# Attention and two expert layers on one core: magnitude from the ratio, range checks moved to the experts, a planner that knows a shared port, three sets of tiles, and a state product in strips

## The chip, the cores and the metric

The kernel runs on one core of a Trainium2 chip. The metric is the device time of one execution in microseconds (us), the median of several runs. A core has a matrix engine (TensorE, PE in the rows), VectorE (DVE), ScalarE (ACT), GpSimd (POOL), and SyncE (SP), which here issues most of the DMAs. Each engine works through its own queue in order, and engines wait for one another by semaphores.

## The reference

Three layers follow one another: an attention with complex decays over 4 batches, 8 heads, 768 steps and 48 columns a head; an expert layer with one dense block; and eight experts of which each token takes two.

```python
mag = np.sqrt(a_re * a_re + a_im * a_im)
scale = np.minimum(mag, 0.999) / (mag + 1e-06)
a_re_n, a_im_n = (a_re * scale, a_im * scale)
for t in range(S):
    new_re = ar * S_re - ai * S_im
    new_im = ar * S_im + ai * S_re
    kv = np.einsum('bhd,bhe->bhde', k[:, :, t], v[:, :, t])
    S_re, S_im = (new_re + kv, new_im)
    y[:, :, t] = np.einsum('bhd,bhde->bhe', q[:, :, t], S_re)
# y as x (3072 x 384): h = x @ w_in; solu = h * softmax(h); layer norm; @ w_out
# then 8 experts, two for each token:
    h = np.maximum(x[mask] @ w1[e], 0.0)
    out[mask] += top2_w[mask, k, None] * (h @ w2[e])
```

## The kernel before

The kernel works in four stages: attention, the dense block (MoE1), the routing, and the experts.

**Attention.** The 768 steps of a batch are cut into chunks of 128, 24 chunks in all. Chunks are handled in groups, 13 of them: two of one chunk at the start and eleven of two (`GROUPS0`, `NG`). `Attention.group` writes the steps of a group. Elementwise work on the decays comes first, on tiles of 128 x 384 for each chunk, so 128 x 768 for most groups: `re` clips the real part and keeps its minimum (L387), `imx` takes the largest imaginary part (L389), `im2` and `re2` square both on ScalarE (L392, L393), `sum` adds the squares on GpSimd (L398), `lnm`, `exm` and `l2c` make the logarithm of the clipped magnitude (L399, L400, L402); beside them `lnre` and `exre` make 1/re, `r` the ratio im/re on GpSimd (L397), and `atan` the angle (L405). Per chunk a triangular matrix product sums the angles over time (`sums`, L414, and `next`, L427) and another the logarithms (`decay`, L440). `f` and `fi` are the decay and its inverse (L443, L445), `qf` and `kf` scale q and k by them on GpSimd (L448, L450), `qp` (GpSimd) and `kp` (VectorE) turn them by cosine and sine into 128 x 768 tiles (L481). Then, per chunk, transposes (`tr`, L494) with copies out of PSUM (`hc`, L499 on ScalarE and L501 on VectorE), the scores `pA` (L506), their mask `aT` (L508), the update of the state `pu` (L515, 20 of the 24 chunks) with `add` and `st` (L521 to L526), and the output `py` (L535), copied by `yc` (L542). py is already written in strips of 32 or 16 rows (`Y_PARTS`).

What checks that the numbers are in range runs along with this: `re`, `imx`, a sum kept by `re2`, and a minimum over the high words of the weights (`wmin`, L310). They are put together in `in_range` at expert 1.

Between the steps of attention stand the conversions of MoE1's weights from pairs of 32-bit words (`plan_convert`, 6 pieces of `w_in` and 8 of `w_out`): L291, L303, L296, L305, L306 on VectorE, and for `w_in` also L308 on GpSimd and L309 on VectorE.

**What sets the order.** Each step is an entry of `Plan` with its engine, a cost from `cost()`, what it reads and writes, a due time, and for loads the time on the wire. `Plan.order` is a list scheduler: it takes the engine that could start first, and of its ready entries the one with the least sum of due time, an offset by name (`OFF`, empty before), `WAIT` times the wait, and `PEN` for a switch of ScalarE's table. The order so found is the order of each engine's queue. `PAIR` says which engine does which step. Tiles of `l2`, `m2` and `an` exist in `EWB` sets.

**MoE1, routing and experts.** TensorE's and ScalarE's order is the order of the code. An expert's work is an up product in 16 steps (`bank`, L1165; `hh` on ScalarE, L1167; `hl` on VectorE, L1168) and a down product over seven tiles (L1179). The weights arrive through SP into tiles r (two buffers `r2` for w2) and are split into a high and a low part (`w2_split`, w2l L1141). Rows of x are gathered and results scattered by GpSimd's DMAs.

Of the kernel before, what the change touches and what calls it, by code (L numbers as in the profile page):

```python
# [21 lines left out]
P = 128  # L22
# [4 lines left out]
VW = HD + D  # L27
# [23 lines left out]
ADVJ = {20: [0, 1, 1, 1]}  # L51
ADV2 = [2, 2, 0, 0, 1, 2, 0, 0]
# [12 lines left out]
EWB = 2  # L65
# [4 lines left out]
NW = D2  # L70
# [3 lines left out]
RE_MIN, IM_MAX, RE2_MAX = 0.55, 0.8, 1e12  # L74
# [6 lines left out]
YM = 0.07  # L81
# [12 lines left out]
def convert(tc, cv, raw_src, n, dst, wmin=None):  # L94

# [33 lines left out]
def moe1_f32(tc, wf, cv, w_in, w_out, g_ln, w_gate, w_noise, wmin=None, plan=None, parts=None):  # L129
# [8 lines left out]
    wm = lambda i: None if wmin is None else wmin[:, i:i + 1]  # L138
# [18 lines left out]
    steps = [small]
    for i in range(NWI):
        d, n = divmod(i * CW, FF)
        steps.append(lambda d=d, n=n, i=i: convert(tc, cv, wi32[d, :, n:n + CW], CW, wi[:, d, n:n + CW], wm(i)))  # L160
# [8 lines left out]
def cost(kind, n):  # L169

    fixed, rate = {"V": (0.15, 960), "VV": (0.15, 530), "VC": (0.18, 750), "V2": (0.2, 720), "G": (0.2, 400), "G1": (0.16, 1200), "A": (0.2, 1200), "AP": (0.17, 1200)}[kind]
    return fixed + n / rate


class Plan:
# [6 lines left out]
    def add(self, fn, engine, us, r=(), w=(), new=(), table=None, due=1e9, wire=0.0, after=(), name="", release=0.0):  # L182
# [24 lines left out]
        self.ops.append((fn, engine, us, deps - {k}, order - {k}, table, due, wire, name, release))  # L207
# [7 lines left out]
    def order(self, trace=None):  # L215
# [21 lines left out]
        table, left, done, wire = None, n, [], 0.0  # L237
        while left:
            e = min((x for x in engines if ready[x]), key=lambda x: max(free[x], min(at[k] for k in ready[x])))
            t = max(free[e], min(at[k] for k in ready[e]))  # L240
            best = None
            for k in ready[e]:
                s = max(t, at[k])
# [32 lines left out]
def plan_convert(plan, tc, cv, raw_src, n, dst, wmin, k, due, release, parts=None):  # L276
# [22 lines left out]
    v = v2 = cost("VC", n)  # L299
    add = lambda fn, us, r, w, new=(), e="V": plan.add(fn, e, us, r=r, w=w, new=new, due=due, release=release, name=f"conv{k}.")  # L300
# [9 lines left out]
    add(lambda: V.tensor_reduce(wmin, hi().bitcast(F32), axis=AX.X, op=ALU.min, apply_absolute_value=True), v, (("raw", k),), ())  # L310


class Attention:


    def __init__(self, tc, x5, y, ident, mask, trt, trc, hpi, le6, magic, remin, immax, resum):
        self.tc, self.x5, self.y, self.ident, self.mask, self.trt, self.trc = tc, x5, y, ident, mask, trt, trc
        self.hpi, self.le6, self.magic = hpi, le6, magic
        self.remin, self.immax, self.resum = remin, immax, resum
        self.t, self.pools = {}, {}  # L320

    def open(self, stack):
# [4 lines left out]
        for x in self.vt:  # L327
            G.memset(x[:, :, HD:], 0.0)
        self.sb = [self.sp.tile([D2, VW], F32, name=f"sb{i}") for i in range(2)]
        for x in self.sb:  # L330
            G.memset(x[:, HD:], 0.0)
# [23 lines left out]
    def group(self, plan, g, b, c0, n, sb, psum, load):  # L355
# [22 lines left out]
        def l_v():  # L378
# [8 lines left out]
        ew(lambda: V.tensor_scalar(re(), re(), RE_MIN, None, op0=ALU.max, op1=ALU.min, accum_out=self.remin[:, g:g + 1]),  # L387
           "V", w=(("ri", g),), name="re")
        ew(lambda: V.tensor_reduce(self.immax[:, g:g + 1], im(), axis=AX.XY, op=ALU.max, apply_absolute_value=True),  # L389
           "V", r=(("im", g), ("ld", g)), name="imx", due=due + 8)  # L390
        m2, l2, an = (lambda: x("m2")), (lambda: x("l2")), (lambda: x("an"))
        ew(lambda: A.activation(sb("l2", g, full, EWB)[:, :n], im(), AF.Square), "A", r=(("im", g), ("ld", g)), new=(("l2", g, EWB),), name="im2")  # L392
        ew(lambda: A.activation(sb("m2", g, full, EWB)[:, :n], re(), AF.Square, accum_out=self.resum[:, g:g + 1]),  # L393
           "A", r=(("ri", g), ("ld", g)), new=(("m2", g, EWB),), extra=.09, name="re2")
        ew(lambda: A.activation(re(), re(), AF.Ln), "A", w=(("ri", g),), table=LNEXP, name="lnre")
        ew(lambda: A.activation(re(), re(), AF.Exp, scale=-1.0), "A", w=(("ri", g),), table=LNEXP, name="exre")
        ew(lambda: eng[E("r")].tensor_mul(sb("an", g, full, EWB)[:, :n], im(), re()), E("r"), r=(("ri", g), ("im", g), ("ld", g)), new=(("an", g, EWB),), name="r")  # L397
        ew(lambda: eng[E("sum")].tensor_add(m2(), m2(), l2()), E("sum"), r=(("l2", g),), w=(("m2", g),), name="sum")  # L398
        ew(lambda: A.activation(l2(), m2(), AF.Ln), "A", r=(("m2", g),), w=(("l2", g),), table=LNEXP, name="lnm")  # L399
# [3 lines left out]
           r=(("m2", g),), w=(("l2", g),), name="l2c")  # L403
# [6 lines left out]
        for i in range(n):  # L410
# [24 lines left out]
            ew(abs_, E("ad", i), r=(("d", g, i), ("d", g), ("an", g)), w=(("ad", g, i),), kind=kinds[E("ad", i)], name=f"ad.{i}.", **one)  # L435
# [8 lines left out]
            def fi_(i=i, pcn=pcn):  # L444
# [904 lines left out]
```

## Time and profile before

| | |
|---|---|
| median of 3 runs | 1017.37 us (1014.77 to 1017.72) |
| profiled execution | 1018.7 us, span 1016.9 us, mean granted clock 0.975 |
| attention | 0 to 278 us |
| MoE1 | 278 to 513 us |
| routing, first gathers | 513 to 569 us |
| experts | 569 to 1016.9 us |

The span is what the trace covers, 1.8 us less than the execution's time. Stages overlap a little at their borders; each border above is the time at which TensorE goes over to the next stage's work.

### The profile page before, as it was taken

The page shows a single profiled execution, that of the slowest core. Times are in us where ns is not written, and L with a number is a line of the kernel's source. Part 1 is how long each engine was busy: PE and PEld are TensorE (multiplying, and loading weights), DVE is VectorE, ACT ScalarE, POOL GpSimd, SP SyncE. Part 2 cuts the span into 40 slices and gives each one's busy share as a digit, 9 for nine tenths or more (in the row PEclk, how much of TensorE's full clock was granted, in tenths as well). Part 3 has the DMA queues.
Part 4 walks back from the last instruction along what each step waited for, and adds up shares of the span by engine and source line. Part 5 has one row for each costly group of instructions (what it writes and reads, how often), then busy time and mean ns, then how long its engine had stood idle before and what let it go on. Part 6 is the DMA issues. An engine that isn't in the chain of part 4 may idle for free.

```text
span 1016.9 us, 17137 instructions
## 1 busy us (share of the span) xinstructions
PE 950.5 (93%) x6599; PEld 847.0 (83%) x6599; DVE 613.6 (60%) x1334; ACT 479.5 (47%) x853; POOL 404.8 (40%) x389
## 2 busy tenths in 40 slices
PE   2887999989899999999969999999999999999995
PEld 1665887767789999899867989999898999989895
DVE  5899998997466778778746355343443534344330
ACT  7787888887445455555423243141322314142220
POOL 4476765765320033033225452343625334362411
PEclk9998999999999999999979999999999999999998
DMA  8444633421000000120023334243432424242300
GB/s 260 154 137 142 205 126 115 136 65 47 10 35 24 16 25 25 39 65 26 17 78 78 105 109 142 60 125 105 118 111 77 143 63 149 90 141 68 94 17 33
DMA packets 65545, 90.89 MB, mean 89 GB/s; under 512 B 24299, under 2 KB 54697, under 8 KB 65456
## 3 DMA queue, kind: packets, MB, share of 16 engines
q1 hardware_dynamic: 53984, 65.02, 21.1%
q0 software_dynamic: 11472, 24.70, 7.8%
q8 instruction: 54, 0.88, 0.4%
q14 instruction: 35, 0.29, 0.1%
HBM read 74.82 MB, written 20.16 MB: 93 GB/s over the span
## 4 chain that ended last, share of the span: by engine, by line
PE 80%; DVE 10%; ACT 4%; DMA 2%; POOL 2%; issue 1%; SPq 1%; POOLq 0%; DVEq 0%; ACTq 0%
PE bank L1179 23%; PE bank L1165 21%; PE px L671 10%; PE ph L622 9%; PE tr L494 4%; PE pA L506 3%; PE py L535 3%; PE pu L515 2%; PE pl L659 2%; PE bank L1023 1%; DVE kp L481 1%; POOL qp L481 1%; PE pth L414 1%; ACT L212 1%; DVE aT L508 1%
## 5 line engine op out<-in xcount | busy, mean ns | idle before, releaser
L1179 PE MATMUL bank<-w2h,hh 128*128 128x384 f32 (+1 forms) x448 | 153.6, 343 | 0.0
L1179 PE MATMUL bank<-w2l,hh 128*128 128x384 f32 (+1 forms) x448 | 150.3, 336 | 0.2 <-DVE w2l L1141 0.2
L1179 PE MATMUL bank<-w2h,hl 128*128 128x384 f32 (+1 forms) x448 | 150.4, 336 | 0.0
L1187 POOL DMA_INDIRECT out_dram<-o,slt x56 | 54.9, 980 | 234.5 <-DVE o L1184 211.4
L1168 DVE SCALAR_TENSOR_TENSOR hl<-bank,hh 128x336 fp32r<-128x336 f32 (+1 forms) x128 | 78.2, 611 | 106.2 <-ACT hh L1167 106.2
L1165 PE MATMUL bank<-xh,w1h 128*128 128x512 f32 (+1 forms) x384 | 136.9, 357 | 0.0
L1165 PE MATMUL bank<-xl,w1h 128*128 128x512 f32 (+1 forms) x384 | 136.1, 354 | 0.2 <-DVE xl L1025 0.2
L1165 PE MATMUL bank<-xh,w1l 128*128 128x512 f32 (+1 forms) x384 | 136.1, 354 | 0.0
L1167 ACT ACTIVATE hh<-bank 128x336 fp32r<-128x336 f32 (+1 forms) x128 | 67.2, 525 | 138.0 <-PE bank L1165 137.1
L961 POOL DMA_INDIRECT sld<-rows,sl x48 | 50.3, 1047 | 186.5 <-DVE sl L958 174.0
L1184 DVE SCALAR_TENSOR_TENSOR o<-bank,slt,gp 128x384 f32<-128x384 f32 (+1 forms) x49 | 30.3, 617 | 126.3 <-PE bank L1179 126.3
L1024 ACT ACTIVATE xh<-bank 128x384 fp32r<-128x384 f32 (+1 forms) x52 | 24.0, 474 | 171.8 <-PE bank L1023 171.8
L1179 PEld LDWEIGHTS bank<-w2l,hh 128*128 128x128 f32 (+1 forms) x448 | 81.7, 182 | 2.1 <-DVE w2l L1141 0.5
L1179 PEld LDWEIGHTS bank<-w2h,hh 128*128 128x128 f32 (+1 forms) x448 | 81.6, 182 | 1.5
L1179 PEld LDWEIGHTS bank<-w2h,hl 128*128 128x128 f32 (+1 forms) x448 | 81.5, 182 | 1.6
L1165 PEld LDWEIGHTS bank<-xl,w1h 128*128 128x128 f32 x384 | 72.5, 189 | 8.0 <-DVE xl L1025 0.5
L1165 PEld LDWEIGHTS bank<-xh,w1l 128*128 128x128 f32 x384 | 72.6, 189 | 7.6
L1165 PEld LDWEIGHTS bank<-xh,w1h 128*128 128x128 f32 x384 | 72.3, 188 | 7.8
L671 PE MATMUL px<-woh,ll 128*128 128x400 f32 x192 | 67.0, 349 | 1.1 <-DVE ll L661 1.0
L671 PE MATMUL px<-woh,lh 128*128 128x400 f32 x192 | 66.8, 348 | 0.7 <-ACT lh L660 0.7
L671 PE MATMUL px<-wol,lh 128*128 128x400 f32 x192 | 66.8, 348 | 0.0
L1003 POOL DMA_INDIRECT x<-x2d,slt x56 | 53.5, 955 | 26.6 <-issue 18.9
(254 smaller groups left out, 2207.1 us busy)
## 6 DMA issues: line engine op xcount, KB each, us to landing
r<-in_moe_w_dram SPq DMA_DIRECT2D x24, 512.0 KB, 3.5
r<-in_moe_w_dram SPq DMA_DIRECT2D x32, 384.0 KB, 3.3
ri<-in_x_dram SPq DMA_DIRECT2D x22, 384.0 KB, 3.8
qk<-in_x_dram SPq DMA_DIRECT2D x22, 384.0 KB, 3.7
out_dram<-zero SPq DMA_DIRECT2D x24, 192.0 KB, 5.7
x2d<-xo SPq DMA_DIRECT2D x24, 192.0 KB, 1.8
vt<-in_x_dram SPq DMA_DIRECT2D x11, 384.0 KB, 3.3
raw<-in_moe_w_out_dram SPq DMA_DIRECT2D x8, 384.0 KB
```

The costliest lines, as they stand in the source:

```text
L494: T.transpose(p[:, h, :], t[dst, g][:, i, 4 * hg + h].rearrange("p a d -> p (a d)"), self.ident)
L506: T.matmul(pA[:, h, :], t["kT", 2 * j + hg][:, h, :], t["qT", 2 * j + hg][:, h, :], start=True, stop=True)
L535: T.matmul(t["py", j][32 * k:32 * k + n1 - n0, d], x[:, h * D + n0:h * D + n1], t[a, 2 * j + h // 4][:, h % 4, :], start=a == "aT", stop=T ...
L622: self.tc.nc.tensor.matmul(ph[:, n:n + 512], l[:, d, :], w[:, d, n:n + 512], start=k == 0, stop=k == 3 * ND - 1)
L671: nc.tensor.matmul(px, a[:, f, :], w[:, f, :], start=k == 0, stop=k == 3 * NF - 1)
L961: ins = G.indirect_dma_start(out=sld, out_offset=bass.IndirectOffsetOnAxis(ap=sl[:, i, kk:kk + 1], axis=0), in_=rows[:, j0 + i, kk, :], in ...
L1003: G.indirect_dma_start(out=x[:m_], out_offset=None, in_=x2d[:rows_known], in_offset=bass.IndirectOffsetOnAxis(ap=o.sl[:m_, i, 0:1], axis=0))
L1165: T.matmul(p[:, :n], wt[:, fs], xx[:, d, :], start=kc == 0, stop=kc == 3 * ND - 1)
L1167: A.activation(o.hh[s][:, f, :], p[:, :n], AF.Relu)
L1168: V.scalar_tensor_tensor(o.hl[s][:, f, :], p[:, :n], 0.0, rd(o.hh[s][:, f, :]), op0=ALU.max, op1=ALU.subtract)
L1179: T.matmul(p[:m_], ht[:, f, c:c + m_], wt, start=kc == 0, stop=kc == 3 * NF - 1)
L1187: si = G.indirect_dma_start(out=out, out_offset=bass.IndirectOffsetOnAxis(ap=o.sl[:m_, i, 2:3], axis=0), in_=t[:m_], in_offset=None, bound ...
```

## The change

- **Magnitude from the ratio.** `re`, `imx`, `im2`, `re2`, `sum` and `lnm` are gone. The logarithm of the squared magnitude is now 2 ln(re) + ln(1 + (im/re)²): `lnre` writes to m2, `rsq` squares the ratio, `lnq` takes the logarithm with a bias of 1 on ScalarE, and `lsum` adds on VectorE.
- **Range checks in the experts.** `range_checks` loads the decays (24 loads of 128 x 2 x 384) and the weights (20 loads) again, into the tiles `r2` that w2 uses, now three buffers, and reduces them on VectorE, one check at every odd step of an up stage from expert 1 on. `in_range` and `objections` move from expert 1 to expert 7.
- **Plan.** `cost()` has other numbers, the steps that use the port shared by GpSimd and VectorE carry a mark (`port`) and wait in the plan until the port is free, and `OFF`, `WAIT`, `PEN`, `ADVJ` and `ADV2` have other numbers. `PAIR`: `qf` alternates between GpSimd and VectorE, and 33 of the 96 copies `hc` are VectorE's instead of 11.
- **Tiles.** `EWB` is 3 instead of 2; qp and kp have one tile for each chunk, three of each (`QB`).
- **State in strips.** A head's product kp by v, 96 rows by 96 columns of which 48 were kept, is now three products of 32 rows by 48 columns. The four parts of py are one entry of the plan.
- The tile of zeros that clears the output has half the columns and is stored twice a row.

```diff
-ADVJ = {20: [0, 1, 1, 1]}
-ADV2 = [2, 2, 0, 0, 1, 2, 0, 0]
+ADVJ = {19: [0, 2, 0, 1], 20: [0, 2, 0, 0]}
+ADV2 = [2, 2, 0, 0, 1, 1, 1, 0]
-PAIR = dict(sum="G", r="G", qf="G", kf="G", qp="G", kp="V", yc="A", hc="AAAAV", d1="V", ad="A")
-OFF = {}
-WAIT = 6
-PEN = 10
+PAIR = dict(r="G", qf="GV", kf="G", qp="G", kp="V", yc="A", hc="AAV", d1="V", ad="A")
+OFF = {"": -31.1, "A": 11.7, "aT": -100.0, "ad": 0.8, "add": -103.1, "atan": -0.6, "ck": 24.4, "conv": 2.9,
...
+WAIT = 39.65
+PEN = 14.57
-EWB = 2
+EWB = 3
+QB = 3
-    fixed, rate = {"V": (0.15, 960), "VV": (0.15, 530), "VC": (0.18, 750), "V2": (0.2, 720), "G": (0.2, 400), "G1": (0.16, 1200), "A": (0.2, 1200), "AP": (0.17, 1200)}[kind]
+    fixed, rate = {"V": (0.15, 960), "VV": (0.15, 960), "V2": (0.15, 1920), "G": (0.4, 541), "GB": (0.55, 550), "G1": (0.3, 1200), "A": (0.2, 1200), "AP": (0.17, 1200)}[kind]
...
-        table, left, done, wire = None, n, [], 0.0
+        table, left, done, wire, port = None, n, [], 0.0, 0.0
+        begin = lambda e, k: max(free[e], at[k], port if ops[k][10] else 0.0)
...
+            if ops[k][10]:
+                port = end[k]
...
-        ew(lambda: V.tensor_scalar(re(), re(), RE_MIN, None, op0=ALU.max, op1=ALU.min, accum_out=self.remin[:, g:g + 1]),
-        ew(lambda: V.tensor_reduce(self.immax[:, g:g + 1], im(), axis=AX.XY, op=ALU.max, apply_absolute_value=True),
-        ew(lambda: A.activation(sb("l2", g, full, EWB)[:, :n], im(), AF.Square), "A", r=(("im", g), ("ld", g)), new=(("l2", g, EWB),), name="im2")
-        ew(lambda: A.activation(sb("m2", g, full, EWB)[:, :n], re(), AF.Square, accum_out=self.resum[:, g:g + 1]),
...
-        ew(lambda: eng[E("sum")].tensor_add(m2(), m2(), l2()), E("sum"), r=(("l2", g),), w=(("m2", g),), name="sum")
-        ew(lambda: A.activation(l2(), m2(), AF.Ln), "A", r=(("m2", g),), w=(("l2", g),), table=LNEXP, name="lnm")
...
+        ew(lambda: A.activation(sb("l2", g, full, EWB)[:, :n], an(), AF.Square), "A", r=(("an", g),), new=(("l2", g, EWB),), name="rsq")
+        ew(lambda: A.activation(l2(), l2(), AF.Ln, bias=self.one), "A", w=(("l2", g),), table=LNEXP, extra=.1, name="lnq")
+        ew(lambda: V.scalar_tensor_tensor(l2(), m2(), 2.0, l2(), op0=ALU.mult, op1=ALU.add), "V", r=(("m2", g),), w=(("l2", g),), kind="VV", port=True, name="lsum")
...
-                        T.matmul(pu[:, h * D:h * D + NW], t["kp", g][:, i, h].rearrange("p a d -> p (a d)"),
-                                 v[:, i, h * D:h * D + NW], start=True, stop=True)
+                        kp = t["kp", j][:, h].rearrange("p a d -> p (a d)")
+                        for m in range(0, D2, 32):
+                            T.matmul(pu[m:m + 32, h * D:(h + 1) * D], kp[:, m:m + 32], v[:, i, h * D:(h + 1) * D],
+                                     start=True, stop=True, skip_group_check=True)
...
-            for parts, hgs in (((0,), (0,)), ((1, 2, 3), (0, 1))):
+            for parts, hgs in ((tuple(range(len(Y_PARTS))), (0, 1)),):
...
+        def decays(n):
+            t = tile_()
+            b, c = divmod(n, NCH)
+            nc.sync.dma_start(t, x5[b, c * P:(c + 1) * P, :2, :])
+            for x, k, op in ((remin, 0, ALU.min), (remax, 0, ALU.max), (immax, 1, ALU.max)):
+                V.tensor_reduce(x[:, n:n + 1], t[:, k], axis=AX.X, op=op, apply_absolute_value=k > 0)
...
-        rb = es.enter_context(tc.tile_pool(name="rb", bufs=2, reuse_waits="tile"))
+        rb = es.enter_context(tc.tile_pool(name="rb", bufs=3, reuse_waits="tile"))
+        checks = range_checks(lambda: rb.tile([P, 2, HD], F32, name="r2"))
...
+                    if f % 2 and checks:
+                        checks.pop(0)()
...
-            if e == 1:
+            if e == E - 1:
                 bad = in_range(bank, ob.tile([P, HD], F32, name="o"))
```

What VectorE has to do around the end of attention, before the change. The lines are those of the kernel before: kp (L481), add (L521), aT (L508), fe (L464), st (L523), a copy (L501), and MoE1's first split `xl` (L612).

```order
L481 TENSOR_TENSOR kp<-qk,sc 128x768
L521 TENSOR_TENSOR pu<-pu,sb_139 96x384
L481 TENSOR_TENSOR kp<-qk,sc 128x768
L508 TENSOR_TENSOR aT<-pA,mask 128x512
L464 COPY fe<-pc 96x16
L523 TENSOR_TENSOR sb_140<-pu,fe 96x384
L501 COPY qT<-tr 96x512
L508 TENSOR_TENSOR aT<-pA,mask 128x512 x3
L612 TENSOR_TENSOR xl<-y,xh 128x384 x2
```

The same place after the change, where L497 is aT, L514 is st, L605 is `xl`, and L292, L304, L297, L306, L307 are a conversion of `w_out`.

```order
L512 TENSOR_TENSOR pu<-pu,sb_132 96x384
L292 TENSOR_SCALAR wt<-raw 128x384
L497 TENSOR_TENSOR aT<-pA,mask 128x512
L514 TENSOR_TENSOR sb_133<-pu,fe 96x384
L304 SCALAR_TENSOR_TENSOR wt<-raw,wt 128x384
L292 TENSOR_SCALAR wt<-raw 128x384
L297 TENSOR_SCALAR wo<-wt 128x384
L304 SCALAR_TENSOR_TENSOR wt<-raw,wt 128x384
L306 SCALAR_TENSOR_TENSOR wo<-raw,wo 128x384
L297 TENSOR_SCALAR wo<-wt 128x384
L307 TENSOR_TENSOR wo<-wt,wo 128x384
L306 SCALAR_TENSOR_TENSOR wo<-raw,wo 128x384
```

Two conversions of `w_out` now stand around the last aT and st; the next row is the first `xl`, and one more row of the conversion follows it.

SP's queue near the start of the program, before the change: loads of decays (ri), of q and k (qk), of v (vt) and of weights (raw), the ends of the decays (fr), and stores of zeros to the output.

```order
L349 DMA ri<-in_x_dram 128x2x384 x2
L918 DMA sld<-pad 128x212
L922 DMA out_dram<-zero 128x384 x8
L349 DMA qk<-in_x_dram 128x2x384 x2
L457 DMA fr<-m_183 8x1x48 x2
L287 DMA raw<-in_moe_w_in_dram 32x1024 x4
L349 DMA ri<-in_x_dram 128x2x384 x2
L349 DMA vt_133<-in_x_dram 128x2x384
L349 DMA qk<-in_x_dram 128x2x384 x2
```

And after it.

```order
L344 DMA ri<-in_x_dram 128x2x384 x2
L907 DMA sld<-pad 128x212
L911 DMA out_dram<-zero 256x1x192 x5
L344 DMA qk<-in_x_dram 128x2x384 x2
L446 DMA fr<-m_161 8x1x48 x2
L288 DMA raw<-in_moe_w_in_dram 32x1024 x4
L344 DMA ri<-in_x_dram 128x2x384 x2
L344 DMA qk<-in_x_dram 128x2x384 x2
L911 DMA out_dram<-zero 256x1x192 x6
L344 DMA vt_129<-in_x_dram 128x2x384
L446 DMA fr<-m_199 16x1x48 x2
L911 DMA out_dram<-zero 256x1x192 x7
```

Of the 24 stores of zeros, 18 now stand up to this row, and 13 of them ahead of loads of v; before, 8 did, and the other 16 came after more than two groups of loads.

VectorE in an up stage of expert 1 after the change, where L1182 is `hl`, L1155 `w2l`, and L1099 the reductions of a check on a tile r. Before the change the rows of `hl` and `w2l` stand there alone.

```order
L1182 SCALAR_TENSOR_TENSOR hl_7492<-bank,hh_7490 128x512
L1155 TENSOR_TENSOR w2l_7509<-r_7506,w2h_7508 128x768
L1182 SCALAR_TENSOR_TENSOR hl_7492<-bank,hh_7490 128x512 x2
L1099 TENSOR_REDUCE remin<-r_7652 128x1
L1099 TENSOR_REDUCE remax<-r_7652 128x1
L1099 TENSOR_REDUCE immax<-r_7652 128x1
L1182 SCALAR_TENSOR_TENSOR hl_7492<-bank,hh_7490 128x512 x2
L1155 TENSOR_TENSOR w2l_7573<-r_7570,w2h_7572 128x768
L1099 TENSOR_REDUCE remin<-r_7681 128x1
L1182 SCALAR_TENSOR_TENSOR hl_7492<-bank,hh_7490 128x512
L1099 TENSOR_REDUCE remax<-r_7681 128x1
L1099 TENSOR_REDUCE immax<-r_7681 128x1
```

So each of the first checks puts three reductions between steps of `hl`.

## Rows read from the trace of the kernel before

**Rows 1.** The page, part 4: shares of the whole span's last chain, by engine.

```profile
PE 80%; DVE 10%; ACT 4%; DMA 2%; POOL 2%; issue 1%; SPq 1%; POOLq 0%; DVEq 0%; ACTq 0%
```

**Rows 2.** Windows: us, busy us (instructions) of PE, PEld, DVE, ACT, POOL, PEclk, DMA, GB/s.

```profile
0.00:278.00 278.00, 236.00 (x2648) 185.34 (x2649) 227.61 (x337) 218.18 (x345) 164.85 (x123) 0.96 0.41 127
580.00:607.70 27.70, 27.53 (x150) 24.40 (x149) 15.41 (x29) 10.71 (x19) 10.91 (x11) 1.00 0.32 94
600.00:900.00 300.00, 300.00 (x1693) 280.80 (x1692) 127.71 (x193) 88.80 (x153) 123.79 (x144) 1.00 0.35 106
```

**Rows 3.** The chain that ended last, 0 to 278 us: shares by line, then pieces.

```profile
by line: PE tr L494 13.0%; PE pA L506 11.5%; PE py L535 10.5%; PE pu L515 7.5%; DVE kp L481 4.9%; POOL qp L481 4.3%; issue 3.9%; PE pth L414 3.6%; ACT L212 3.2%; DVE aT L508 3.0%; PE pc L440 2.7%; PE pth L427 2.6%; DMA vt<-in_x_dram 2.3%; D
386 pieces in order of time: start us, us, what
...
34.43 2.11 DVE wt L303
...
42.61 1.36 PE pu L515 x16
...
215.99 1.04 DVE wo L296
...
262.75 2.55 DVE kp L481
```

**Rows 4.** By tile or line: ns min/median/max, first and last start in us.

```profile
L481 DVE TENSOR_TENSOR kp<-qk,sc x24: 939/1142/2578, 24.6 to 262.8; 128x768 f32<-128x768 f32 x24
...
L481 POOL TENSOR_TENSOR qp<-qk,sc x24: 1809/2288/3501, 23.4 to 262.7; 128x768 f32<-128x768 f32 x24
...
L303 DVE SCALAR_TENSOR_TENSOR wt<-raw,wt x14: 543/718/2192, 15.5 to 241.1; 128x384 int32<-128x384 int32 x8, 128x512 int32<-128x512 int32 x6
...
L309 DVE TENSOR_TENSOR wil<-w,wih x6: 675/679/2110, 27.3 to 124.3; 128x512 fp32r<-128x512 f32 x6
...
L389 DVE TENSOR_REDUCE immax<-ri x13: 548/939/947, 3.7 to 204.0; 128x1 f32<-128x768 f32 x11, 128x1 f32<-128x384 f32 x2
```

**Rows 5.** Groups by line and shape, 0 to 278 us: busy us, mean ns.

```profile
L481 POOL TENSOR_TENSOR qp<-qk,sc 128x768 f32<-128x768 f32 x24 | 56.0, 2336 | 10.3 <-issue 4.8 <-ACT sc L473 1.7 <-POOL qk L450 1.1
...
L212 ACT ACT_TABLE_LOAD x33 | 42.3, 1283 | 0.6
L481 DVE TENSOR_TENSOR kp<-qk,sc 128x768 f32<-128x768 f32 x24 | 35.9, 1498 | 2.5 <-POOL qk L450 1.6 <-ACT sc L473 0.6 <-issue 0.3
...
L499 ACT ACTIVATE kT<-tr 96x512 f32<-96x512 f32 x48 | 28.4, 591 | 27.0 <-PE tr L494 26.5
...
L448 POOL TENSOR_TENSOR qk<-qk,m 128x384 f32<-128x384 f32 x24 | 27.2, 1132 | 20.3 <-ACT m L443 19.1 <-DVE wo L306 1.1
...
L398 POOL TENSOR_TENSOR m<-m,l 128x768 f32<-128x768 f32 x11 | 22.7, 2062 | 26.0 <-ACT l L392 21.3 <-DMA raw<-in_moe_w_in_dram 4.7
...
L402 DVE SCALAR_TENSOR_TENSOR l<-l,m 128x768 f32<-128x768 f32 x11 | 13.0, 1179 | 0.0
...
L399 ACT ACTIVATE l<-m 128x768 f32<-128x768 f32 x11 | 9.3, 846 | 0.0
...
L501 DVE COPY qT<-tr 96x512 f32<-96x512 f32 x11 | 7.4, 676 | 0.0
```

**Rows 6.** Timeline of TensorE: two neighbouring parts of py, eight records each.

```profile
276.50 0.40 PE L535 MATMUL py<-qT,sb 96*32 96x128 f32 x8
276.72 0.40 PE L535 MATMUL py<-aT,vt 128*32 128x128 f32 x8
```

**Rows 7.** TensorE's waits, 0 to 60 and 510 to 570 us: total, times, longest.

```profile
PE pc L440 <- DVE l L402: 10.5, 1, 10.5
...
PE ph L1023 <- DVE xl L1025: 4.3, 2, 3.1
```

**Rows 8.** Timeline of VectorE: the first split of MoE1, with its idle time.

```profile
278.79 0.56 DVE L612 TENSOR_TENSOR xl<-y,xh 128x384 fp32r<-128x384 f32 x1 [2.58 <-ACT xh L611]
```

**Rows 9.** The page, part 6: loads of expert weights, KB and us to landing.

```profile
r<-in_moe_w_dram SPq DMA_DIRECT2D x32, 384.0 KB, 3.3
```

More of the change, by code (lines that the diff above doesn't have):

```diff
@@ L26 @@
 HD = H * D
-VW = HD + D
+VW = HD
 NT = B * NCH
@@ L56 @@
 SCAN = .66
-PAIR = dict(sum="G", r="G", qf="G", kf="G", qp="G", kp="V", yc="A", hc="AAAAV", d1="V", ad="A")
-OFF = {}
-WAIT = 6
-PEN = 10
+PAIR = dict(r="G", qf="GV", kf="G", qp="G", kp="V", yc="A", hc="AAV", d1="V", ad="A")
+OFF = {"": -31.1, "A": 11.7, "aT": -100.0, "ad": 0.8, "add": -103.1, "atan": -0.6, "ck": 24.4, "conv": 2.9,
+       "cos": -13.4, "cq": 12.1, "d": -2.4, "decay": -2.0, "ends": 25.1, "endt": -15.0, "exm": -0.2, "exre": -6.0,
+       "f": 0.1, "fe": 12.4, "fi": 0.1, "kf": -46.2, "kp": 1.0, "lc": -5.4, "lda": -14.7, "ldq": -16.6, "ldv": 4.3,
+       "ldw": 15.9, "lnq": -3.1, "lnre": 1.3, "lsum": -12.4, "next": 5.2, "pu": 13.5, "qf": -1.9, "qp": -74.2,
+       "r": -23.2, "rsq": 8.1, "sin": -0.3, "st": 26.9, "sums": -4.9, "trk": 1.6, "trq": -69.4, "y": -118.9,
+       "yc": -20.8}
+WAIT = 39.65
+PEN = 14.57
 DELTA = 0.1
@@ L180, in __init__, with add @@
         self.readers = {}
-    def add(self, fn, engine, us, r=(), w=(), new=(), table=None, due=1e9, wire=0.0, after=(), name="", release=0.0):
+    def add(self, fn, engine, us, r=(), w=(), new=(), table=None, due=1e9, wire=0.0, after=(), name="", release=0.0, port=False):
         k = len(self.ops)
@@ L206, in add @@
             self.readers.setdefault(x, []).append(k)
-        self.ops.append((fn, engine, us, deps - {k}, order - {k}, table, due, wire, name, release))
+        self.ops.append((fn, engine, us, deps - {k}, order - {k}, table, due, wire, name, release, port or engine == "G"))
     def emit(self, nc):
@@ L298, in plan_convert @@
     out = lambda: t["dst"] if parts else dst
-    v = v2 = cost("VC", n)
-    add = lambda fn, us, r, w, new=(), e="V": plan.add(fn, e, us, r=r, w=w, new=new, due=due, release=release, name=f"conv{k}.")
+    v, v2 = cost("VV", n), cost("V2", n)
+    add = lambda fn, us, r, w, new=(), e="V": plan.add(fn, e, us, r=r, w=w, new=new, due=due, release=release, name=f"conv{k}.", port=True)
     plan.add(load, "S", .47 * len(raw_src), new=(("raw", k, CVB),), wire=1.46 * n / CW, due=due - 4, release=max(release - 8, 0.0), name=f"ldw{k}")
@@ L849, in body @@
     V.memset(le6, math.log(2e-6))
+    one = const.tile([P, 1], F32, name="one")
+    V.memset(one, 1.0)
     magic = const.tile([P, 1], F32, name="magic")
@@ L892, in body @@
     cv = wst.enter_context(tc.tile_pool(name="cv", bufs=CVB, side="right"))
-    wmin = const.tile([P, NWI + NF], F32, name="wmin")
     wi_parts = [keep.tile([P, ND, FF], F32R, name=n) for n in ("wih", "wil")]
     plan = Plan()
-    wfs = moe1_f32(tc, wf, cv, w_in, w_out, g_ln, w_gate, w_noise, wmin, plan, wi_parts)
+    wfs = moe1_f32(tc, wf, cv, w_in, w_out, g_ln, w_gate, w_noise, plan, wi_parts)
     with ExitStack() as at:
-        att = Attention(tc, x5, y, ident, mask, trt, trc, hpi, le6, magic, remin, immax, resum)
+        att = Attention(tc, x5, y, ident, mask, trt, trc, hpi, le6, one, magic)
         att.open(at)
@@ L918, in body @@
     nc.sync.dma_start(sld.rearrange("(p n) w -> p n w", p=P), pad)
-    zero = const.tile([P, HD], F32, name="zero")
+    zero = const.tile([P, HD // 2], F32, name="zero")
     G.memset(zero, 0.0)
     for j in range(NT):
-        nc.sync.dma_start(out[j * P:(j + 1) * P], zero)
+        nc.sync.dma_start(out[j * P:(j + 1) * P].rearrange("p (a d) -> p a d", a=2),
+                          zero[:, None, :].to_broadcast([P, 2, HD // 2]))
     nz = const.tile([P, NT, E], F32, name="nz")
```

111 lines of the change are left out of this document (53 added, 58 removed).

## The prediction

> **What bounds the kernel now.** I read the page's chain first: over the whole span it is TensorE for 80%, with VectorE 10%, ScalarE 4%, GpSimd 2% [rows 1]. The table by stretch says where those others sit. In the experts TensorE is busy 300.00 us of 300 at a granted clock of 1.00; nothing that helps another engine helps there, it can only hurt. In the attention stage (0 to 278 us) TensorE is busy 236.00 of 278, VectorE 227.61, ScalarE 218.18 and GpSimd 164.85 [rows 2]: four engines, none full, so the order and the waits between them set its length. All of the change but the moved range checks lies there.
>
> The chain of that stage has 386 pieces [rows 3]. Adding them by engine, I get about 144 us of TensorE, 56 of VectorE, 27 of ScalarE, 18 of GpSimd and 15 of DMA; the rest is issue. The header gives kp on VectorE 4.9% (13.5 us, in 8 pieces), qp on GpSimd 4.3% (11.9 us, in 4), pu 7.5% (20.7 us), table loads 3.2% (8.8 us). Fifteen more pieces, 19.7 us in all, are conversions of MoE weights on VectorE and the magnitude's `l2c`; the first and the last of them are shown.
>
> These durations are not one number. kp takes 0.94 us at least and 2.58 at most for the same tile; qp 1.81 to 3.50. A reduction like `imx` has no such spread: 0.55 for the half tile and 0.94 for the whole, never above 0.95 [rows 4]. The last kp and the last qp begin within 0.1 us of each other (262.8 and 262.7), and that kp takes 2.55 us [rows 3, 4]. I read it so: VectorE operations with two operands in SBUF, or in their fast form, and GpSimd's wait for one another, and other VectorE operations don't. That is the shared port which the change plans with. Its price on the chain: kp 13.5 less 8 × 0.94 = 6.0; qp 11.9 less 4 × 1.81 = 4.7; the fifteen others 19.7 less 8.3 at the shortest duration of each form (0.54 us for L303 on 384 columns, 0.68 for L309 on 512) = 11.4. Together 22 us of waiting.
>
> **The change, part by part.** The sum is made against the profiled execution, 1018.7 us, 1.3 above the median of the runs shown.
>
> *Port waits.* GpSimd loses 13 `sum` (22.7 us for the 11 whole ones) and 12 of 24 `qf` (12 × 1.13 = 13.6) [rows 5], about 38 us that held the port at observed lengths. VectorE gains 12 `qf` and 13 `lsum`, which also take it, some 18 us. So demand falls, and the planner now starts one such operation at a time, with a third set of tiles to choose among. Bounds: nothing (the real order leaves the planned times within a few us) and -22 (every wait on the chain gone). I take **-13**: demand falls by about a tenth at uncontended lengths, which alone is worth 2, and the rest is the plan; a removed wait also exposes the next chain, and TensorE at 85% is near.
>
> *State in strips.* One pu was 16 records in 1.36 us [rows 3], the last 20 of 24 chunks' worth. It becomes 48 records of 32 rows by 48 columns, spread over three column strips. The nearest row is py, which already runs in strips: eight records start every 0.22 us, 27.5 ns each, with 128 columns [rows 6]. If py's pace is that of its columns, 48 records cost 48 × 27.5 × 48/128 × 4/3 = 0.66 us (three strips instead of four side by side); if it is a floor for each record, 48 × 27.5 = 1.32. I take 1.0: 0.36 × 20 × 0.76 (20.7 of the 27.2 us are on the chain) = **-5**, bounds -11 and 0. The Trainium skill ("TensorE: Matmul & The Clock Gate", section "Wait — 56ns, not 53.3ns?") says that starts of matmuls never come closer than about 25 ns however few the columns; by it, as an estimate, a pu is 48 × 25 = 1.2 us, this term would be -2.5 and the time 2.5 us later. py's rows at 27.5 ns cannot tell it from streaming, so it is a bound here and not the value.
>
> *ScalarE.* Three passes a group (`im2`, `re2`, `lnm`) give way to two (`rsq`, `lnq`): 13 × about 0.8 = -10.3 us. 22 of the copies after the transposes go to VectorE: 22 × 0.59 = -13.0. Three fewer table loads: -3.8 [rows 5]. That is 27 of ScalarE's 218 us, one eighth; one eighth of its 27 us on the chain is **-3.5** (bounds 0 and -6).
>
> *VectorE's own count.* Gone: 13 `re` (as long as `imx`, 11 × 0.94 + 2 × 0.55, and their accumulator reads, 12.5), 13 `imx` (11.4), 14 weight reductions (at 0.55 or a little more, 8). Added: 13 `lsum` at the shortest of `l2c`'s (11.5), 12 `qf` at about 0.54 (6.5), 22 copies at 0.68 (14.9). 31.9 out, 32.9 in [rows 4, 5]. Nothing is won in busy time, but what went could always run beside GpSimd, and much of what came can't: at the contended mean of `l2c` (1.18) and a contended qf it is 7 us more. **0**, bounds -6 and +7.
>
> *The start.* TensorE's first work waits 10.5 us for `l2c` [rows 7]. The new magnitude goes through a logarithm, an exponential, the ratio on GpSimd, a square, a logarithm and one more VectorE pass before it, one dependent pass more than before, while `re` and `imx` leave VectorE's queue ahead of it. On SP's queue 18 of the 24 zero stores now stand in rows 18 to 27 of its order, 13 of them ahead of the first loads of v, where 8 stood before. **+1**, bounds 0 and +4.
>
> *Attention to MoE1.* Before, VectorE was idle 2.58 us ahead of the first `xl` [rows 8]. Now eight operations of two `w_out` conversions stand between the last aT and it: 8 × 0.55 at most when nothing contends, 4.4, less those 2.58 of idle time: **+2**, bounds 0 and +4. Between MoE1 and the experts, where TensorE waits 4.3 us in two for the experts' first `xl` [rows 7], the edits leave the chain as it is but for some loads of slots that SP issues behind three weight loads: **0**, bounds -2 and +2.
>
> *Checks in the experts.* In the stretch of one up stage VectorE is busy 15.41 of 27.70 us [rows 2]. An expert gets 8 checks, of which about 14 reductions, 7.7 us, stand in that stage: 23 of 27.7, so it still fits behind TensorE, and later experts have none. Their loads are 384 KB like those of w2, which land in 3.3 us [rows 9], against about two steps of `hl` (27.7/16 = 1.7 us each) between issue and use, and PSUM banks that let TensorE run a step ahead, 1.7 more: 5.1. **+0.5**, bounds 0 and +10. If that cover is gone, VectorE waits at a reduction, `hl` stands behind it, and TensorE waits for `hl`.
>
> Sum: -13 - 5 - 3.5 + 0 + 1 + 2 + 0 + 0.5 = **-18**, so 1000.7 for a profiled execution like this one, and 1.3 less, 999.4, for the median.
>
> **The rivals.**
>
> *R1, VectorE stays what it is.* Work moved between GpSimd and VectorE meets the same port, the order on the chip drifts from the plan, and only the strips and ScalarE pay: -5 - 3.5 + 3.5 = -5, so 1013.7 profiled, about 1012. For it: 32.9 us added against 31.9 removed, and the added part contends. Against it: 38 us less on GpSimd. The Trainium skill ("Perfetto Trace Analysis", section "Optimizing Scalar/DVE Operations") says this of such moves: GpSimd and VectorE share a read port, so that shifting work between them might not help. The spread of kp and qp agrees that there is such a port.
>
> *R2, TensorE becomes the bound in attention.* All waits go, and the stage is its first 10.5 idle us plus 236 busy less 7 for the strips: 239.5 instead of 278, -38.5, so 980.2 profiled, about 979. Against it: phase, decay and state are chains through four engines at every group, and the clock in the stage is 0.96 already.
>
> *R3, slower: checks land late.* Three experts carry the 24 decay checks, each with 384 KB in r2 buffers that w2 uses too. Once a load lands later than the 5.1 us above, each further us is paid 24 times; from 0.75 us further on that eats the whole 18. At 6.3 us it takes 1.2 × 24 = 29: about 1028. For it: the loads share SP's queue with those of w1 and w2. Against it: 3.3 us landing in the rows, a third buffer.
>
> *R4, the change doesn't do what it says.* The planner's times are off, the third tiles stay unused, and what is saved comes back as waits elsewhere: within 3 us of 1017.
>
> **How the numbers follow.** Forecast 0.58, R1 0.17, R2 0.10, R3 0.07, R4 0.08. The forecast's own range is 988 to 1009, about half of the way to the bounds of the two large terms, ports and strips. For 8 in 10 I add R1 and half of R2: 979 to 1014. A measurement here tells about 0.3% from nothing, 3 us. Faster: 0.58 + most of R1 (0.13) + R2 = 0.80 (rounded); same: rest of R1 and most of R4, 0.10; slower: R3 and a little of R4, 0.10.
>
> **What would show it.** Port: the mean of kp falls from 1.50 towards 1.0 us and of qp from 2.34 towards 1.9; if both stay, R1. Strips: pu's 48 records in 0.7 to 1.3 us. ScalarE: 190 us busy in attention. Attention should end near 258; at 240 it is R2, at 272 R1, at 278 R4. Experts: TensorE 100% with no wait for `hl`; a wait of VectorE for r2's load is R3. The end of attention: the first `xl` 2 us later behind y than before. The prediction is wrong above all if the port's 22 us was not what the stage waited for, and another chain of the same length lies under it.

## The result, and the profile after

The changed kernel takes 1000.96 us (median of 4 runs, 999.84 to 1001.53) against 1017.55 for the kernel before beside it: a ratio of 0.984, 95% interval 0.9825 to 0.9855. The profiled execution has a span of 999.8 us, 17.1 less than before. The prediction was 999.4.

The stages tell more than the sum. First the attention stage and a stretch of the experts after the change, in the windows view: length, busy us of TensorE, its weight loads, VectorE, ScalarE, GpSimd, then granted clock, DMA share and GB/s; they answer to [rows 2].

```profile
0.00:254.90 254.90, 214.00 (x3298) 168.00 (x3298) 196.32 (x330) 193.94 (x296) 113.66 (x93) 0.96 0.46 139
600.00:700.00 100.00, 100.00 (x577) 94.68 (x576) 57.66 (x102) 27.93 (x48) 34.58 (x43) 1.00 0.47 152
```

Then the first matmuls of MoE1 and of the experts after the change, and under them before; the first start is where a stage begins.

```profile
L615 PE MATMUL ph<-wih,xh x144: 387/389/628, 254.9 to 483.4; 128*128 128x512 f32 x144
L1179 PE MATMUL bank<-xh,w1h x384: 308/356/482, 512.5 to 958.6; 128*128 128x512 f32 x96, 128*128 128x336 f32 x96
```

```profile
L622 PE MATMUL ph<-wih,xh x144: 389/389/641, 279.0 to 501.0; 128*128 128x512 f32 x144
L1165 PE MATMUL bank<-xh,w1h x384: 314/353/628, 530.4 to 976.1; 128*128 128x512 f32 x96, 128*128 128x336 f32 x96
```

MoE1 begins 24.1 us earlier, the experts only 17.9 earlier, and the end 17.1: from MoE1's first matmul to the experts' it was 251.4 us and is 257.6. So attention gave 24, and the 257 us behind it took 6.2 back.

Attention's chain after the change, header and pieces (start, us, what), as in [rows 3]:

```profile
by line: PE tr L483 13.7%; PE pA L495 12.9%; PE py L526 11.7%; PE pc L429 6.7%; PE pth L416 5.3%; PE pu L506 4.6%; PE pth L403 4.4%; DMA fr<-m 4.2%; issue 3.4%; DVE kp L470 3.0%; DVE l L391 2.6%; DVE aT L497 2.6%; DMA raw<-in_moe_w_in_dram 
...
61.34 4.92 DMA fr<-m
...
70.73 1.92 DVE l L391
...
245.95 4.42 DMA raw<-in_moe_w_out_dram
```

Adding the pieces by engine, GpSimd fell from 17.6 to 1.8 us, ScalarE from 26.7 to 9.6, VectorE from 55.7 to 52.6; TensorE rose from 144 to 153 and DMA from 15 to 26. New on the chain is `fr`, the 3 KB transfers of the ends of the decays, with 10.6 us in three pieces. TensorE's own waits for `fr` are no longer than before, 4.9 us against 4.7.

The durations that answer to [rows 4, 5] (ns min/median/max, first and last start; then groups with busy us and mean ns):

```profile
L470 DVE TENSOR_TENSOR kp<-qk,sc x24: 940/949/2594, 26.2 to 240.1; 128x768 f32<-128x768 f32 x24
...
L470 POOL TENSOR_TENSOR qp<-qk,sc x24: 1817/1858/2604, 23.1 to 240.4; 128x768 f32<-128x768 f32 x24
```

```profile
L470 POOL TENSOR_TENSOR qp<-qk,sc 128x768 f32<-128x768 f32 x24 | 48.1, 2011 | 46.7 <-issue 18.6 <-DVE qk L437 15.8 <-DVE qT L490 3.9
L210 ACT ACT_TABLE_LOAD x31 | 39.8, 1283 | 1.3 <-PEq L1352 0.8
...
L470 DVE TENSOR_TENSOR kp<-qk,sc 128x768 f32<-128x768 f32 x24 | 27.7, 1155 | 0.2 <-issue 0.2
```

kp's median is now 0.949 us, close to its minimum of 0.940: most kp wait for nothing. The state product in the timeline of TensorE, and the operation behind it:

```profile
66.52 0.88 PE L506 MATMUL pu<-vt,kp 128*32 128x48 f32 x48
67.33 0.91 PE L403 MATMUL pth<-an,trt 128*128 128x384 f32 x2
```

A pu takes 0.81 us to the next start; it was 1.36 [rows 3].

Where the 6.2 us went shows in TensorE's waits late in MoE1, after the change (300 to 490 us) and before (325 to 505):

```profile
PE pT L935 <- DVE ohs L923: 2.3, 2, 2.1
PE pT L937 <- DVE csum L925: 1.6, 2, 1.2
```

```profile
PE pT L947 <- DVE csum L935: 0.7, 2, 0.5
PE pT L945 <- DVE ohs L933: 0.2, 1, 0.2
```

These are the matmuls of a routing step. The first matmuls of tile 21 of MoE1 are 22.4 us ahead of before (455.86 against 478.25), those of tile 23 only 17.7 (479.86 against 497.51): 4.7 us are lost in two tiles. Another 1.3 us went at tile 2, where TensorE waits 2.6 us for the first `ll`, 1.0 us before. From tile 23's first matmul to the experts' it is 32.6 us, before 32.9.

### The profile page after: what moved, and what is told of

It is laid out like the page before. It is cut to its first block, busy times and chain, and to the rows that moved or that the text cites. A ratio compares the mean times of both kernels' runs of the same rounds, so it can differ in the third digit from the quotient of the medians.

```text
span 999.8 us, 18486 instructions
## 1 busy us (share of the span) xinstructions
PE 930.2 (93%) x7239; PEld 830.7 (83%) x7239; DVE 618.1 (62%) x1421; ACT 454.8 (45%) x802; POOL 355.0 (36%) x359
## 4 chain that ended last, share of the span: by engine, by line
PE 76%; DVE 13%; DMA 4%; ACT 3%; issue 2%; POOL 0%; SPq 0%; POOLq 0%; DVEq 0%
PE bank L1193 22%; PE bank L1179 21%; PE px L664 8%; PE ph L615 7%; PE tr L483 3%; PE pA L495 3%; PE py L526 3%; PE pc L429 2%; PE bank L1013 2%; PE pth L416 1%; PE pu L506 1%; PE pl L652 1%; PE pth L403 1%; DMA fr<-m 1%; DVE p L628 1%
## 5 line engine op out<-in xcount | busy, mean ns | idle before, releaser
L1182 DVE SCALAR_TENSOR_TENSOR hl<-bank,hh 128x336 fp32r<-128x336 f32 (+1 forms) x128 | 75.4, 596 | 66.2 <-ACT hh L1181 66.1
L1014 ACT ACTIVATE xh<-bank 128x384 fp32r<-128x384 f32 (+1 forms) x52 | 24.1, 474 | 171.4 <-PE bank L1013 171.4
L470 POOL TENSOR_TENSOR qp<-qk,sc 128x768 f32<-128x768 f32 x24 | 48.1, 2011 | 46.7 <-issue 18.6
```

What stands on the lines that cost most here:

```text
L470: eng[e].tensor_mul(o, heads(s[:, i])[:, :, None, :].to_broadcast([P, H, 2, D]), t["sc", g][:, i])
L1182: V.scalar_tensor_tensor(o.hl[s][:, f, :], p[:, :n], 0.0, rd(o.hh[s][:, f, :]), op0=ALU.max, op1=ALU.subtract)
```

## The experiments

The runs were made in three groups: e1, e2, e3 and e5; e4, e6, e7 and e8; e9, e10, e12 and e13. The kernel before ran in each, with medians of 1017.5, 1030.3 and 1036.8 us, so each run is given as a ratio to before in its own group. The changed kernel itself was run only for the result above. Where a run of the second or third group is set against its 0.984, that this ratio carries over is assumed.

**e1, the routing tables of before.**

```diff
-ADVJ = {19: [0, 2, 0, 1], 20: [0, 2, 0, 0]}
-ADV2 = [2, 2, 0, 0, 1, 1, 1, 0]
+ADVJ = {20: [0, 1, 1, 1]}
+ADV2 = [2, 2, 0, 0, 1, 2, 0, 0]
```

> The changed kernel with ADVJ and ADV2, the tables that say after which parts of a MoE1 tile and of the first up stage a routing step is issued, as before the change. In the trace after the change TensorE waits 2.09 us for ohs and 1.17 for csum in tile 21 of MoE1, which before took 0.26, and the lead over the kernel before falls from 22.4 us at tile 21 to 17.7 at tile 23. Theory A: the steps are now issued before VectorE can have done them, and these tables cost about 4 us: about 997 us, ratio to before 0.980. Rival B: the lead is lost because the stage ahead is shorter and something that came from outside (slots, stores, VectorE's own queue) has not caught up; the tables do nothing: about 1001, ratio 0.984.

Measured: 992.99 us, ratio 0.9765 (0.9738 to 0.9792), 8 us better than the changed kernel. TensorE's waits for routing in MoE1 (300 to 486 us) are those of before again:

```profile
PE pT L937 <- DVE csum L925: 0.7, 2, 0.5
...
PE pT L935 <- DVE ohs L923: 0.2, 1, 0.2
```

```profile
L615 PE MATMUL ph<-wih,xh x144: 387/393/774, 251.6 to 475.7; 128*128 128x512 f32 x144
L1179 PE MATMUL bank<-xh,w1h x384: 308/355/479, 504.0 to 949.4; 128*128 128x512 f32 x96, 128*128 128x336 f32 x96
```

From MoE1's first matmul to the experts' it is 252.3 us, 5.3 of the 6.2 come back, and 4.7 of them in tiles 21 and 22. Rival B falls. Tile 21 tells the same in all other traces but e4's: from its first matmul to the next tile's it takes 13.0 to 15.2 us with the new tables and 9.3 with the old. The rest of the 8 us is attention, which ended 3 us earlier in this execution with the same order; the tables don't explain that.

**e2, whole state products.**

```diff
-                        for m in range(0, D2, 32):
-                            T.matmul(pu[m:m + 32, h * D:(h + 1) * D], kp[:, m:m + 32], v[:, i, h * D:(h + 1) * D],
-                                     start=True, stop=True, skip_group_check=True)
+                        n = min(D2, HD - h * D)
+                        T.matmul(pu[:, h * D:h * D + n], kp, v[:, i, h * D:h * D + n], start=True, stop=True)
```

> The changed kernel with the state product in whole 96-row products of 96 columns, as before the change (the last head 48 columns), and the plan's order kept. One pu took 1.36 us before and takes 0.81 from its start to the next operation's after. Theory A: about 0.55 x 20 x 0.75 = 8 us lost, ratio to before 0.992. Rival B: TensorE has slack in attention (40 of 255 us idle), so the waits absorb it: under 3 us lost, ratio 0.984 to 0.987.

Measured: 0.9881 (0.9859 to 0.9903), 4.2 us lost, between the two. The pu that took 0.81 us above is 1.40 us long again:

```profile
66.36 1.56 PE L506 MATMUL pu<-vt,kp 128*96 128x96 f32 x16
67.76 0.88 PE L403 MATMUL pth<-an,trt 128*128 128x384 f32 x2
```

Most of the 20 take 1.32 us, so about 20 × 0.51 = 10 us of TensorE are at stake, and some two fifths of it show in the time.

**e3, the plan of before.** Costs, WAIT, PEN as before, OFF empty, no port; all else as after.

```diff
-WAIT = 39.65
-PEN = 14.57
+OFF = {}
+WAIT = 6
+PEN = 10
...
-            if ops[k][10]:
-                port = end[k]
```

> The changed kernel, with the planner's costs, WAIT, PEN and empty OFF as before and no port in the plan; all operations, engines and tiles as after. Theory A: the plan is worth the larger part of the 22 us of port waits: 10 to 16 us lost, ratio to before 0.994 to 1.000, and the mean of kp back near 1.4 us. Rival B: less work on GpSimd and ScalarE does it whatever the order: under 4 us lost, ratio 0.984 to 0.988, kp near 1.15.

Measured: 1.0093 (1.0073 to 1.0113): 26 us lost against the changed kernel, and 0.9% slower than before. MoE1 begins at 279.7 us, as late as before the change, so attention's gain is gone. kp and MoE1's first matmuls, by tile:

```profile
L463 DVE TENSOR_TENSOR kp<-qk,sc x24: 939/2037/2595, 22.9 to 265.4; 128x768 f32<-128x768 f32 x24
L608 PE MATMUL ph<-wih,xh x144: 388/390/776, 279.7 to 508.5; 128*128 128x512 f32 x144
```

kp's median is 2.04 us where before had 1.14, its mean 1.80 against 1.50: kp waits more than before. Theory A holds and was too small. But the old plan costs more than waits at the port. In e3's chain of attention (0 to 279 us) the table loads, L205, are 18.5 us (2.6 in the changed kernel) and the issues of stores of zeros, L904, 13.4 us (none there); SP's queue shows twenty of these stores in one run, ahead of a load of v and of an `fr`. The chain's header, the table loads of the whole program (31 in the changed kernel), and SP's queue:

```profile
by line: PE tr L476 14.1%; PE pA L488 10.3%; issue 7.0%; ACT L205 6.6%; PE py L519 5.1%; DVE kp L463 5.0%; SPq L904 4.8%; POOL qp L463 4.3%; PE pu L499 3.5%; DMA qk<-in_x_dram 3.2%; DMA raw<-in_moe_w_in_dram 2.9%; PE pth L409 2.6%; DVE aT L
...
L205 ACT ACT_TABLE_LOAD x45 | 57.7, 1283 | 1.5 <-PEq L1345 0.8
...
56.47 14.13 SPq L904 DMA_DIRECT2D out_dram<-zero  x20
70.69 0.57 SPq L337 DMA_DIRECT2D vt<-in_x_dram  x1
```

So e3 shows what the whole plan is worth, and not what its port rule is.

**e9 and e10, the two halves of the plan.** e9 has the new costs and the port rule with OFF, WAIT and PEN as before. e10 has everything new but the rule; its edit is:

```diff
-            if ops[k][10]:
-                port = end[k]
```

> The changed kernel with the planner's new costs and its rule that one operation holds the port at a time, but OFF empty, WAIT 6 and PEN 10 as before. With the whole plan as before the ratio was 1.009, with the whole new one 0.984. Theory A (knowing the port is most of it): 0.986 to 0.994, kp's median near 0.95 us. Rival B (the table of offsets and weights is most of it, found for these very costs): 0.998 to 1.009.

> The changed kernel with the new costs, OFF, WAIT and PEN, but without the rule that the port is held by one operation at a time. Theory A (knowing the port is most of it): 0.996 to 1.010, kp's median well over 1.1 us. Rival B (the offsets carry the order even so): 0.984 to 0.992.

Measured: 0.9944 (0.991 to 0.9977) and 1.000 (0.997 to 1.003). kp in e9, then in e10:

```profile
L465 DVE TENSOR_TENSOR kp<-qk,sc x24: 944/948/2361, 26.4 to 249.2; 128x768 f32<-128x768 f32 x24
```

```profile
L468 POOL TENSOR_TENSOR qp<-qk,sc 128x768 f32<-128x768 f32 x24 | 56.4, 2365 | 45.3 <-DVE aT L495 9.7 <-issue 8.7 <-DVE d L410 8.0
...
L468 DVE TENSOR_TENSOR kp<-qk,sc 128x768 f32<-128x768 f32 x24 | 36.9, 1549 | 0.7 <-ACT sc L460 0.6
```

With the rule most kp wait for nothing; without it the mean is 1.55 us, as before the change [rows 5] (the median, 0.96, is not what Theory A expected). Of the 2.5% between the old plan (e3) and the new, costs and rule alone bring 1.5 (e9), and the table on top of them 1.0; costs and table without the rule bring 0.9 (e10). The rule by itself is worth 1.6%, from e10's 1.000 to the changed kernel's 0.984; in e10's own group e12 below, with the rule and two sets of tiles, is at 0.9816. e9 lies on the edge of Theory A's range, e10 inside it; Rival B falls in both.

**e5, no checks.**

```diff
-                    if f % 2 and checks:
-                        checks.pop(0)()
+    for x, v in ((remin, 0.9), (remax, 0.9), (immax, 0.1), (wmin, 1.0)):
+        V.memset(x, v)
```

> The changed kernel without the 44 loads and the reductions of the range checks in the experts; the minima and maxima are set to constants, so the test of the ranges is left out of the computation. Theory A: the checks are hidden, 0 to 1 us gained, ratio 0.983 to 0.984. Rival B: their reductions or loads hold hl or the weights up in some steps: 3 us or more gained, ratio 0.981 or less.

Measured: 0.9828 (0.9798 to 0.9857), not to be told from 0.984. The interval reaches into Rival B's range, but the traces decide: from the experts' first matmul to the end it is 487.3 us with the checks and 487.4 without. In the changed kernel VectorE does wait for the checks' loads (540 to 1000 us; total, times, longest):

```profile
DVE remin L1099 <- DMA r<-in_x_dram: 29.0, 15, 4.6
DVE wmin L1104 <- DMA r<-in_moe_w_in_dram: 15.4, 11, 3.5
DVE wmin L1104 <- DMA r<-in_moe_w_out_dram: 15.1, 8, 3.2
```

That is 59 us of waiting, and from 600 to 900 us TensorE is busy all of the time all the same.

**e6, the stores of zeros after attention, and e7, that with e1's tables.**

```diff
-    G.memset(zero, 0.0)
+    V.tensor_scalar(zero, y[:, NT - 1, :HD // 2], 0.0, None, op0=ALU.mult)
```

> The changed kernel, with the tile of zeros made from the last chunk of y times 0, so that its 24 stores come after attention instead of in SP's first 40 rows; nothing else of attention changes. In the trace after the change seven of these stores hold SP for 6.1 us and the next ends of decays (fr) land 4 us or later after their issue, with three waits of TensorE of 4.9 us in all, and the first aT is at 42.9 us against 33.7 before. Theory A: the stores delay the loads and fr: 4 us or more gained, ratio to before 0.976 to 0.980. Rival B: the late start is the longer magnitude chain and the plan's own order: under 2 us gained, ratio 0.982 to 0.986.

> The late zeros together with ADVJ and ADV2 as before the change; the version that should beat both kernels. If both work and add up: ratio to before about 0.972, 989 us; if the stores do nothing, that of the old tables alone, 0.9765 (0.974 to 0.979), 993 us.

Measured: 0.9834 (0.98 to 0.9869) and 0.9789 (0.9752 to 0.9827). The stores were not what delays the start: the first aT is at 43.9 us, no earlier. The tables seem to be worth 0.45% here too, but the intervals overlap.

**e8, qf and the copies on the engines of before.**

```diff
-PAIR = dict(r="G", qf="GV", kf="G", qp="G", kp="V", yc="A", hc="AAV", d1="V", ad="A")
+PAIR = dict(r="G", qf="G", kf="G", qp="G", kp="V", yc="A", hc="AAAAV", d1="V", ad="A")
```

> The changed kernel with all qf on GpSimd and the copies shared as before (AAAAV), the plan made anew with its numbers as after. Theory A: with the port planned for, taking 12 us off GpSimd and 13 off ScalarE is worth some us: 3 to 8 lost, ratio to before 0.987 to 0.992. Rival R1 of the prediction, weak form: moving work between GpSimd and VectorE is worth nothing: within 3 us, ratio 0.981 to 0.987.

Measured: 0.9846 (0.9802 to 0.989). No loss can be seen: the weak form of R1 is what happened, with the reserve that the interval holds Theory A's smaller values and that the table of offsets was not made for this PAIR.

**e4, two sets of tiles, then e12, that with a table load at the end of attention, and e13, e12 with e1's tables.**

```diff
-EWB = 3
+EWB = 2
...
             self.ops[k][0]()
+        nc.scalar.preload_act_table_set(LNEXP)
```

> The changed kernel with two sets of l2, m2 and an (EWB 2), the plan made anew with its numbers as after. Theory A (the plan's order is what pays, and it needs tiles to choose among): 5 to 10 us lost, ratio to before 0.989 to 0.994. Rival B: the third set is not used by the order that matters: within 3 us of the changed kernel, ratio 0.981 to 0.987.

> Two sets of l2, m2 and an as before the change, with ScalarE's table for logarithm and exponential loaded once more after the last step of attention. The run with two sets alone ended attention 9 us earlier than the changed kernel and lost 70 us in MoE1 to 55 table loads of 1.28 us, since its last attention step left the table for sine there. Theory A (two sets cost nothing; the loads were the loss): ratio 0.972 to 0.980. Rival B (attention's gain is paid back in MoE1 in another way): 0.984 or more.

> The same with ADVJ and ADV2 as before the change, the version that should beat both kernels: 4 to 5 us less than with two sets alone, ratio to before 0.967 to 0.976 if both add up.

Measured: 1.0347 (1.0309 to 1.0385), 0.9816 (0.9783 to 0.9848) and 0.9804 (0.9765 to 0.9843). e4 is a lesson in reading stages: its attention is shorter than with three sets (MoE1 begins at 245.5 us, in e6 and e8 of the same group at 252.6 and 254.6). Then MoE1 loads ScalarE's tables again and again, 53 times, and takes 320.9 us; the largest groups of loads by line:

```profile
L639 ACT ACT_TABLE_LOAD x24 | 30.8, 1283 | 0.4
L638 ACT ACT_TABLE_LOAD x20 | 25.7, 1283 | 0.4
L685 ACT ACT_TABLE_LOAD x7 | 9.0, 1283 | 0.1
```

With one load of the other table after attention (e12), MoE1 begins at 248.0 us, no load follows, and the ratio is no worse than the changed kernel's. So the third set buys nothing in these plans. e12's total lies between its two theories, and e13 gains too little over e12 to be told from nothing: its tile 21 is 5.7 us shorter, but from tile 23 to the experts it takes 35.4 us instead of 32.5. Of all kernels e1 has the best ratio.

## Why the prediction was right, point by point

- **Port waits, -13.** By the same sum as in the prediction (pieces of the chain above their shortest duration), 8 to 9 us of the 22 are left: -13 to -14. That the plan does it, and not the lower demand, is shown by runs with the same operations: the sum is about 19 us under the old plan (e3), 25 without the rule (e10) and 5 with costs and rule alone (e9). The plan is worth more than these waits, though. Of the 26 us that e3 loses, much is table loads and stores of zeros on the chain, which the prediction didn't price. Under the old plan the edits together bring attention nothing: it ends at 279.7 us, before at 279.0.
- **Strips, -5.** A pu is 0.81 us, not 1.0; the time moves by 4.2 (e2). That is nearer to py's streaming bound, 0.66, than to its floor per record, 1.32: 48 records start within 0.81 us, 17 ns each. The Trainium skill ("TensorE: Matmul & The Clock Gate", section "Wait — 56ns, not 53.3ns?") gives its floor of about 25 ns from one matmul's start to the next. A matmul of the program has two records here: the 0.81 us are 34 ns for each of 24 matmuls, above that floor, and 17 ns for each of 48 records, below it. I had applied it to the records, so the estimate of 1.2 us by it was too long.
- **ScalarE, -3.5.** Its busy time fell by 24 us, and its share of the chain by 17. Yet e8, which gives the copies back to it, loses nothing that can be told. How much of attention's 24 us is the dropped passes was not measured by itself.
- **VectorE's own count, 0.** Its busy time fell by 31 us, from 227.6 to 196.3, but its work did not: with every operation at the shortest duration of its form the sum is 198 us before and 195 after. What went is waiting, 51 us above those durations before and 20 after.
- **The start, +1.** Mis-sized: the first aT is at 42.9 us instead of 33.7.

```profile
L497 DVE TENSOR_TENSOR aT<-pA,mask x48: 671/691/692, 42.9 to 250.7; 128x512 f32<-128x512 f32 x48
```

```profile
L508 DVE TENSOR_TENSOR aT<-pA,mask x48: 673/691/694, 33.7 to 275.5; 128x512 f32<-128x512 f32 x48
```

The plan's order does it, not the stores (e6: 43.9) nor the longer chain of operations: with the same operations it is 29.7 under the old plan (e3) and 32.3 with the port rule and an empty OFF (e9). The lead comes later, 16 us at chunk 6.
- **Attention to MoE1, +2.** From the last aT to the first `xl` it is 4.2 us (250.71 to 254.94) instead of 3.3: +1. The chain puts a load of w_out, 4.42 us, ahead of the last aT; but VectorE is not idle there, so that this load cost time is not shown.
- **MoE1 to the experts, 0.** For the stretch that I named it holds: from MoE1's last tile to the experts it is 32.6 us instead of 32.9. What failed is the step ahead of it, that all of the change but the range checks lies in attention, so that MoE1's tiles had no term. ADVJ stands in the diff, and it sends routing's matmuls to TensorE before VectorE has their operands. That costs about 5 of the 6.2 us lost (e1). The 1.3 us near the start of MoE1 are not the tables': tiles 1 and 2 take 22.8 us in e1, 22.9 in the changed kernel and 21.6 before. Their cause stays open.
- **Checks, +0.5.** It is 0.8 us longer from the experts' first matmul on, but e5, without the checks, has that too, so they cost nothing. R3 stayed away although the mechanism is there: VectorE waits 59 us for their loads, all within the cover.

So the total came within 2 us of 999.4 by two misses of about 6 us that cancel: attention gave 24.1 instead of 18.5, MoE1 took 6.2 back instead of nothing. That closeness is luck; the main mechanism, waits at the port that the plan removes, is not. Of the rivals, R2 is refuted (TensorE still idles 41 of 255 us), and so are R4 and the strong form of R1, by the time itself and by the means of kp and qp, which fell to 1.16 and 2.01 us. Part of both is true: the third set of l2, m2 and an is not needed (e12), and without the new plan the edits together save nothing (e3).

## What to carry to other kernels

Where two engines wait for one another at a port, as GpSimd and VectorE do here, a planner that only counts each engine's time makes them meet: kp's median was 2.04 us in e3 and 0.95 when the plan let one operation hold the port at a time. That rule was worth 1.6% here (e10 against the changed kernel), while the operations removed and moved brought nothing under the old plan. Offsets tuned for one set of operations belong to it: change the tiles or the plan's last step, and look again at what state it leaves (the table on ScalarE) to the stage behind. A table of steps in a later stage is part of the change too: read which engine will wait at each step that it pulls forward.

## What the hardware showed that was not expected

- Attention's length differs between executions of the same order by some us: MoE1 began at 254.9, 251.6 (e1) and 252.8 us (e5). Part of it can be seen. Near 65 us the changed kernel falls 1.3 us behind e1 where TensorE waits for an `fr`, 3 KB issued behind stores of zeros of 192 KB each, which landed after 5.3 us instead of 4.1. And from 110 to 160 us the granted clock (the third number from the end) is lower; the changed kernel, then e1:

```profile
110.00:160.00 50.00, 43.67 (x762) 34.64 (x761) 39.43 (x61) 42.30 (x64) 25.57 (x20) 0.97 0.48 149
```

```profile
110.00:160.00 50.00, 42.09 (x719) 33.50 (x717) 40.63 (x66) 42.84 (x64) 26.35 (x20) 1.00 0.50 154
```

Whether these make the whole difference was not tested.
- In e4 the last table that attention loads is the one for sine, at 220.0 us. MoE1 then has 53 loads of 1.283 us and the experts two, as logarithm and exponential call for two tables in turn there. With the table for both loaded after attention (e12) there is none.
